# Linear attention on one core: no block and no closing barrier, and the first load in two transfers

## The chip, the cores and the metric

The kernel runs on one core of one Trainium2 chip. The metric is the device time of one execution in microseconds. Each execution also has a *span*, from the first to the last instruction in its trace. The metric is longer than the span; the difference is called "outside the span" below.

## The reference

```python
phi_q = where(q > 0, q + 1, exp(q)) + 1e-6      # q, k, v: 1 x 32 x 2048 x 128, bf16
phi_k = where(k > 0, k + 1, exp(k)) + 1e-6
kv  = einsum("bhsd,bhse->bhde", phi_k, v);  z = phi_k summed over s
out = einsum("bhqd,bhde->bhqe", phi_q, kv) / (einsum("bhqd,bhd->bhq", phi_q, z)[..., None] + 1e-6)
```

## The kernel before

For each of 32 heads, q, k and v come in as one transfer each of 128 rows of 4 KB (512 KB). PE transposes q; ACT takes the exponentials (`eq`, `ek`) and a relu; DVE and POOL do the rest of phi and copy v; PE forms kv and the result; DVE divides; one 512 KB store goes out per head (the last in three parts). Every engine runs a fixed list of operations. SP issues every transfer. These are the parts that the change and the argument touch (`# ...` marks cuts):

```python
WARM = (15, 4, 4)              # warm-up matmuls: w2 and w1 (4 + 4) run before the first transposes
ORDER = {
    "PE": "w2 w1 T0.0 T0.1 w0 kv0.0 kv0.1 ...",
    "SP": "ldq0.0 ldk0.0 ldv0.0 ldk1.0 ldq1.0 ...",
}
# ...
def load(name, dst, src, h, i, t0, t1, last):
    add("SP", f"ld{name}{h}.{i}", lambda e: e.dma_start(dst[:, h % NI, t0:t1], rows(src, h)[:, t0:t1]),
        last, dma=f"{name}{h % NI}.{i}")
# ... the first transposes wait for ldq0 and for the identity that POOL builds
block = es.enter_context(nc.Block())

@block.gpsimd
def _(e):
    pr.emit("POOL", e)

@block.sync
def _(e):
    pr.emit("SP", e)
    for s in range(NO):                       # 12 output buffers; the last store uses o7
        if f"o{s}" in pr.count:
            e.wait_ge(pr.get(f"o{s}"), pr.count[f"o{s}"])
# ... the same for scalar, tensor, vector; the block ends in a drain and a barrier of all engines
```

## Time and profile before

| | before |
|---|---|
| time, median of the first 3 runs | 171.89 us |
| span of the profiled run (its time was 171.16) | 169.3 us |
| last store issued, last landing, end of span | 165.52, 168.53, 169.26 us |

The page begins with the span and the busy time of each engine. PE, DVE and ACT are all above 90%, so no share tells what a change at either end is worth.

```profile
span 169.3 us, 6317 instructions
...
PE 158.8 (94%) x2775; PEld 153.5 (91%) x2775; DVE 153.5 (91%) x267; ACT 153.7 (91%) x133; POOL 85.8 (51%) x71
```

The table of windows gives, for each stretch, its length, the busy time of each engine, the granted clock, the busy share of the DMA engines and what they moved. From 12 us on both ACT and the DMA engines are full; the last two columns of the first rows show how soon the DMA stream gets to speed.

```profile
core 0: us, PE busy (x) PEld busy (x) DVE busy (x) ACT busy (x) POOL busy (x), PEclk, DMA share, GB/s
2.00:3.00 1.00, 1.00 (x4) 0.36 (x3) 0.00 (x0) 0.02 (x1) 0.00 (x0) 1.00 0.92 319
3.00:7.00 4.00, 4.00 (x28) 2.19 (x27) 0.47 (x2) 1.66 (x2) 1.27 (x1) 1.00 1.01 397
7.00:12.00 5.00, 4.86 (x57) 3.43 (x55) 2.88 (x11) 5.00 (x7) 1.79 (x3) 1.00 1.02 415
12.00:150.00 138.00, 136.15 (x2469) 135.42 (x2470) 135.43 (x229) 137.22 (x118) 79.52 (x60) 1.00 1.03 413
```

The timeline of SP's queue at the start (start, duration): each issue keeps the queue for about 0.4 us, and the second load goes out at 1.16. The first packets of q0 move at 1.87.

```profile
0.74 0.37 SPq L324 DMA_DIRECT2D la<-in_q_dram  x1
1.16 0.42 SPq L324 DMA_DIRECT2D la<-in_k_dram  x1
1.63 0.42 SPq L324 DMA_DIRECT2D la<-in_v_dram  x1
```

The timeline at the start, ACT's first activation and POOL's first instruction inside the block (the memset that begins the identity); in brackets, how long the engine had been idle and what ended that. The activation is what the first transposes release.

```profile
0.73 0.20 POOL L300 MEMSET la<- 128x128 bf16 x1 [0.29 <-POOLq L468]
...
5.34 1.02 ACT L372 ACTIVATE la<-la 128x1024 bf16<-128x1024 bf16 x1 [3.32 <-PE la L368]
```

The instructions of SP's closing waits (L442) and of the end of the block (L253): count, duration in ns, first and last start. The last landing is at 168.53; everything that starts after it is what the block's end costs.

```profile
L442 SPq EVENT_SEMAPHORE  x6: 17/28/28, 167.2 to 168.8; - x6
```

```profile
L253 SPq COMPARE_BRANCH  x1: 38/38/38, 168.9 to 168.9; - x1
L253 SPq DRAIN  x1: 7/7/7, 169.0 to 169.0; - x1
L253 SPq EVENT_SEMAPHORE  x1: 17/17/17, 169.2 to 169.2; - x1
L253 ACTq EVENT_SEMAPHORE  x1: 17/17/17, 169.2 to 169.2; - x1
```

### The profile page before, as it was taken

Reading aid. Unit: us, or ns where it says so; the run is one execution under the profiler, and the core shown is the slowest. Engines: PE = TensorE matmul, PEld = TensorE weight load, DVE = VectorE, ACT = ScalarE, POOL = GpSimd, SP = SyncE. Lnnn points to the kernel's source line nnn. Section 1 sums busy time; section 2 is a strip of 40 time slices with the busy share of each in tenths; the row PEclk is TensorE's granted clock in tenths of the full one; section 3 lists DMA queues with packets and bytes.
Section 4 is the critical chain, followed back from the end, with each engine's and each line's share of the span. In section 5 each row is a group of like instructions: output and inputs, shape, how many; then the busy total and the mean of one; then the engine's idle time right before and its main releaser. Section 6 shows DMA issues by size and latency. Waiting matters only on the chain.

```text
span 169.3 us, 6317 instructions
## 1 busy us (share of the span) xinstructions
PE 158.8 (94%) x2775; PEld 153.5 (91%) x2775; DVE 153.5 (91%) x267; ACT 153.7 (91%) x133; POOL 85.8 (51%) x71
## 2 busy tenths in 40 slices
PE   6997999999999999999999999999999999999850
PEld 2576989999999999999999999999999999999740
DVE  0178989999999999999999999999999999999891
ACT  3799989999999999999999999999999999995800
POOL 1446546655665456545566555554565555635000
PEclk9999999999999999999999999999999999999999
DMA  5999999999999999999999999999999999999984
GB/s 204 394 420 415 403 407 410 406 410 410 413 410 410 410 411 407 410 408 419 411 415 417 413 423 411 411 419 408 415 417 414 417 413 419 415 412 420 391 342 175
DMA packets 18748, 67.53 MB, mean 399 GB/s; under 512 B 2080, under 2 KB 2464, under 8 KB 18720
## 3 DMA queue, kind: packets, MB, share of 16 engines
q1 hardware_dynamic: 18720, 67.12, 98.5%
q8 instruction: 22, 0.36, 0.8%
q14 instruction: 6, 0.05, 0.1%
HBM read 50.33 MB, written 16.78 MB: 396 GB/s over the span
## 4 chain that ended last, share of the span: by engine, by line
PE 86%; DVE 6%; ACT 4%; issue 1%; DVEq 0%; POOL 0%; POOLq 0%
PE la L357 33%; PE la L394 19%; PE la L396 17%; PE la L368 15%; DVE la L410 4%; ACT la L336 2%; PE la L315 2%; ACT la L372 1%; PE la L389 1%; DVE la L374 1%; DVE la L403 1%; ACT la L378 1%; DVE la L342 0%; DVEq L253 0%; ACT la L362 0%
## 5 line engine op out<-in xcount | busy, mean ns | idle before, releaser
L410 DVE TENSOR_TENSOR la<-la 128x1536 bf16<-128x1536 f32 (+2 forms) x65 | 77.6, 1195 | 0.3
L396 PE MATMUL la<-la 128*128 128x129 bf16 x512 | 68.1, 220 | 0.0
L394 PE MATMUL la<-la 128*128 128x129 bf16 x512 | 68.1, 219 | 0.0
L372 ACT ACTIVATE la<-la 128x2048 bf16<-128x2048 bf16 (+2 forms) x35 | 60.4, 1731 | 5.0 <-PE la L368 3.3
L357 PE MATMUL la<-la 128*128 128x129 bf16 x1024 | 64.0, 219 | 0.0
L336 ACT ACTIVATE la<-la 128x2048 bf16<-128x2048 bf16 (+1 forms) x33 | 61.3, 1861 | 0.0
L350 POOL COPY la<-la 128x1024 int32<-128x1024 int32 (+1 forms) x33 | 40.3, 1223 | 40.1 <-DVE la L403 30.5
L357 PEld LDWEIGHTS la<-la 128*128 128x128 bf16 x1024 | 60.0, 97 | 0.5 <-POOL la L350 0.5
L346 POOL TENSOR_SCALAR la<-la 128x1024 bf16<-128x1024 bf16 x32 | 44.9, 1403 | 28.2 <-DVE la L410 24.2
L396 PEld LDWEIGHTS la<-la 128*128 128x128 bf16 x512 | 49.5, 97 | 0.0
L394 PEld LDWEIGHTS la<-la 128*128 128x128 bf16 x512 | 47.1, 97 | 0.0
L389 PE MATMUL la<-la 128*128 128x3 bf16 (+1 forms) x192 | 32.3, 168 | 3.4 <-DVE la L410 1.9
L368 PE MATMUL la<-la 128*128 128x128 bf16 x512 | 33.7, 219 | 0.0
L378 ACT ACTIVATE la<-la 128x1024 bf16<-128x1024 bf16 (+1 forms) x32 | 33.5, 1046 | 0.0
L368 PEld LDWEIGHTS la<-la 128*128 128x128 bf16 x512 | 29.2, 97 | 0.9 <-DMA la<-in_q_dram 0.2
L339 DVE TENSOR_SCALAR la<-la 128x2048 bf16<-128x2048 bf16 (+1 forms) x33 | 23.5, 716 | 3.1 <-ACT la L336 3.0
L389 PEld LDWEIGHTS la<-la 128*128 128x128 bf16 x192 | 18.7, 97 | 4.4 <-DVE la L410 2.3
L374 DVE TENSOR_SCALAR la<-la 128x2048 bf16<-128x2048 bf16 (+2 forms) x35 | 21.9, 625 | 0.1
L381 DVE TENSOR_SCALAR la<-la 128x1024 bf16<-128x1024 bf16 x31 | 20.8, 672 | 0.2 <-ACT la L372 0.2
L342 DVE TENSOR_SCALAR la<-la 128x1024 bf16<-128x1024 bf16 x32 | 14.2, 447 | 5.3 <-DMA la<-in_k_dram 5.3
L403 DVE RECIPROCAL la<-la 128x12 f32<-128x12 f32 (+2 forms) x65 | 12.8, 198 | 2.9 <-ACT la L362 1.0
L362 ACT ACTIVATE la<-la 128x129 bf16<-128x129 f32 x32 | 9.0, 282 | 0.8 <-PE la L357 0.8
(14 smaller groups left out, 11.7 us busy)
## 6 DMA issues: line engine op xcount, KB each, us to landing
la<-in_q_dram SPq DMA_DIRECT2D x32, 512.0 KB, 15.4
la<-in_k_dram SPq DMA_DIRECT2D x32, 512.0 KB, 15.3
la<-in_v_dram SPq DMA_DIRECT2D x32, 512.0 KB, 15.4
out_dram<-la SPq DMA_DIRECT2D x31, 512.0 KB, 15.3
out_dram<-la SPq DMA_DIRECT2D x2, 192.0 KB, 2.8
out_dram<-la SPq DMA_DIRECT2D x1, 128.0 KB, 3.0
```

What stands on the lines that cost most here:

```text
L336: add("ACT", f"ek{h}.{i}", lambda e, a=a, b=b: e.activation(em_sb[:, h % NE, a:b], k_sb[:, h % NI, a:b], ACT.Exp), over("ldk", h, ld_parts ...
L346: add("POOL", f"rkp{h}.{i}", lambda e, a=a, b=b: e.tensor_scalar(rk_sb[:, h % NR, a:b], k_sb[:, h % NI, a:b], BIG, 0.0, op0=ALU.min, op1=A ...
L350: add("POOL", f"v1{h}.{i}", lambda e, a=a, b=b: e.tensor_copy(v1_sb[:, h % NV, a:b, 0:D].bitcast(i32), v_sb[:, h % NI, a:b].bitcast(i32)), ...
L357: ins = e.matmul(kv_ps, lhsT=src[:, j], rhs=v1_sb[:, h % NV, j, 0:NC], start=(j + part == 0), stop=(j == NT - 1 and part == 1))
L368: ins = e.transpose(xT[:, j], q_sb[:, h % NI, j], ident[:])
L372: add("ACT", f"eq{h}.{i}", lambda e, a=a, b=b: e.activation(emq_sb[:, h % NQ, a:b], xT[:, a:b], ACT.Exp), over("T", h, t_parts, a, b) + fr ...
L374: add("DVE", f"emq{h}.{i}", lambda e, a=a, b=b: e.tensor_scalar(emq_sb[:, h % NQ, a:b], emq_sb[:, h % NQ, a:b], 1.0, EPS, op0=ALU.min, op1 ...
L378: add("ACT", f"rqa{h}", lambda e: e.activation(rq_sb[:, h % NQ, 0:n], xT[:, 0:n], ACT.Relu), over("T", h, t_parts, 0, n) + freed(NQ, h, (" ...
L389: e.matmul(_ap(o_ps[:, :], o + D, [[NC, m]]), lhsT=ones[:], rhs=epsr[:, 0:m], start=True, stop=False, skip_group_check=True)
L394: e.matmul(to, lhsT=emq_sb[:, h % NQ, t], rhs=kvs_sb[:, h % NK], start=False, stop=False, skip_group_check=True)
L396: ins = e.matmul(to, lhsT=rq_sb[:, h % NQ, t], rhs=kvs_sb[:, h % NK], start=False, stop=True, skip_group_check=True)
L410: return e.tensor_tensor(out=_ap(o_sb[:, :, :, :], first(o_sb[:, h % NO, t0, 0:1]) - first(o_sb[:, :, :, :]), [[m * D, nb], [D, m], [1, D] ...
```

## The change

Its intent: save the branches into and out of the block and the barrier at its end, and let the DMA engines start sooner with a small first transfer (16 of the 128 rows of q0). The waits at the end are put in an order in which the last store's comes last.

```diff
 WARM = (15, 4, 4)
+FIRST = "ldq0.0"
     "SP": """
-        ldq0.0 ldk0.0 ldv0.0 ...
+        first ldq0.0 ldk0.0 ldv0.0 ...
         def load(name, dst, src, h, i, t0, t1, last):
-            add("SP", f"ld{name}{h}.{i}", lambda e: e.dma_start(dst[:, h % NI, t0:t1], rows(src, h)[:, t0:t1]),
+            p0 = 0
+            if f"ld{name}{h}.{i}" == FIRST:
+                p0 = 16
+                add("SP", "first", lambda e: e.dma_start(dst[:p0, h % NI, t0:t1], rows(src, h)[:p0, t0:t1]), dma="first")
+            add("SP", f"ld{name}{h}.{i}", lambda e: e.dma_start(dst[p0:, h % NI, t0:t1], rows(src, h)[p0:, t0:t1]),
                 last, dma=f"{name}{h % NI}.{i}")
 # (the first transposes also wait for "first")
-        block = es.enter_context(nc.Block())
-        @block.gpsimd
-        def _(e):
-            pr.emit("POOL", e)
-        # ... and so on for each engine, with SP's waits for o0 to o11 in that order
+        for e, engine in (("POOL", nc.gpsimd), ("SP", nc.sync), ("ACT", nc.scalar), ("PE", nc.tensor), ("DVE", nc.vector)):
+            pr.emit(e, engine)
+        last = f"o{(NH - 1) % NO}"
+        for name in [f"o{s}" for s in range(NO) if f"o{s}" in pr.count and f"o{s}" != last] + [last]:
+            nc.sync.wait_ge(pr.get(name), pr.count[name])
```

More of the change, by code (lines that the diff above doesn't have):

```diff
@@ L132 @@
     "SP": """
-        ldq0.0 ldk0.0 ldv0.0 ldk1.0 ldq1.0 ldv1.0 ldk2.0 ldk3.0 ldq2.0 ldv2.0 ldq3.0 ldk4.0 ldv3.0 ldv4.0 ldk5.0
+        first ldq0.0 ldk0.0 ldv0.0 ldk1.0 ldq1.0 ldv1.0 ldk2.0 ldk3.0 ldq2.0 ldv2.0 ldq3.0 ldk4.0 ldv3.0 ldv4.0 ldk5.0
         ldq4.0 ldk6.0 ldv5.0 ldq5.0 ldk7.0 ldv6.0 ldv7.0 ldq6.0 ldk8.0 ldq7.0 ldv8.0 ldk9.0 ldq8.0 ldq9.0 ldv9.0
@@ L369, in g @@
                     return ins
-                add("PE", f"T{h}.{i}", g, over("ldq", h, ld_parts, a, b) + ["ident"] + ((every("eq", h - 1, q_parts) + rqs(h - 1)) if h else []))
+                add("PE", f"T{h}.{i}", g, over("ldq", h, ld_parts, a, b) + (["first"] if h == 0 else []) + ["ident"] + ((every("eq", h - 1, q_parts) + rqs(h - 1)) if h else []))
             for i, (a, b) in enumerate(q_parts(h)):
@@ L430, in bass_standalone__linear_attn_elu__prompt_kernel @@
             pr.get(name)
-        block = es.enter_context(nc.Block())
-        @block.gpsimd
-        def _(e):
-            pr.emit("POOL", e)
-        @block.sync
-        def _(e):
-            pr.emit("SP", e)
-            for s in range(NO):
-                if f"o{s}" in pr.count:
-                    e.wait_ge(pr.get(f"o{s}"), pr.count[f"o{s}"])
-        @block.scalar
-        def _(e):
-            pr.emit("ACT", e)
-        @block.tensor
-        def _(e):
-            pr.emit("PE", e)
-        @block.vector
-        def _(e):
-            pr.emit("DVE", e)
+        for e, engine in (("POOL", nc.gpsimd), ("SP", nc.sync), ("ACT", nc.scalar), ("PE", nc.tensor), ("DVE", nc.vector)):
[3 more added lines that the diff above has]
+            nc.sync.wait_ge(pr.get(name), pr.count[name])
 _INS = ['q', 'k', 'v']
```

## The prediction

> **What bounds the kernel now.** Time 171.89 us; profiled span 169.3. In the table of windows, from 12 to 150 us, ACT is busy 137.2 of 138 us, PE 136.2, and the DMA engines move 413 GB/s without a pause. At the start the chain of waits is: POOL builds the identity (0.73 to 1.47), eight warm-up matmuls (3.33 us), the first transposes at 4.7, ACT's first activation at 5.34; ACT then hardly stops until 160.2. The first load (q0) is issued at 0.74, its first packets move at 1.87, its last landing is at 4.08: 0.1 to 0.2 us before the warm-up lets the transposes start. At the end DVE stops at 165.5; the last store, issued at 165.52, lands at 168.53. The last stores land every 1.25 us, the slowest DMA engine never idle, so DMA sets the end as much as DVE.
>
> **What the change removes, adds and moves.**
>
> 1. End. SP sees the last landing at 168.55. Then come four waits already satisfied (0.06 each), a compare-and-branch at 168.87, a drain at 169.04 and a five-engine barrier to 169.26: 0.71 us, all on the critical path. The change puts the last store's wait last and has no branch, drain or barrier, so the span should end within 0.05 us of the last landing. Gain 0.7 us. The runtime's own wait for all engines ("Runtime: NRT & Kernel Launch", the preamble/postamble breakdown, about 1.5 us) stays, outside the span; this trace does not show it. The metric is some 2 us longer than the span, so I assume that it counts the program's end and passes the 0.7 us on.
>
> 2. Start, branches. Between the opening barrier's release (SP 0.67, POOL 0.63) and the first issue (0.74) or memset (0.73) stands one branch. Without it I expect 0.03 to 0.08 us earlier on both; POOL's is on the path through the warm-up to ACT.
>
> 3. Start, the split. The first issue took 0.37 us; packets started 1.13 us after it began. Estimate: 16 rows still cost 0.2 to 0.35 us of issue, since stores of 1, 1.5 and 4 KB rows all take 0.33. The first packets come perhaps 0.1 to 0.2 us earlier, for 64 KB (0.16 us at 410 GB/s), but the 112 rows and all later loads are issued 0.2 to 0.35 us later, their packets at about 2.1. "DMA: Bandwidth & Descriptors" (section on the semaphore increment of 16, how many engines) gives the largest common divisor up to 16, so both parts use all 16 engines. The stream's opening packets are slow (205 to 411 ns against 159); the small transfer may absorb that. Net on the DMA stream: -0.2 to +0.15 us. One more wait for the first transposes, free unless q0 lands after 4.2.
>
> Nothing else changes order. On the critical path lie 0.7 us at the end and about 0.1 at the start.
>
> **Prediction: 171.0 us, 8 in 10 between 170.5 and 171.6.** Faster by over 2%: 0.01; within 2%: 0.98; slower: 0.01.
>
> **What would show it.** Span about 168.5; no drain or barrier after the last landing; POOL's memset and SP's issue 0.03 to 0.08 us earlier; first packets at 1.6 to 1.8; q0 landed at 3.9 to 4.2; first activation at 5.25 to 5.3; last landing 168.2 to 168.6.
>
> **What would make it wrong.** The time may exclude the closing barrier, leaving 0.1 us. The second issue may delay the bulk and so q0 past the warm-up. The instruction-fetch packets (22 of 16 KB, about 1.05 us each) may fall on other DMA engines and move the last landing by up to 1 us either way.

## More of the kernel before

The waits of ACT from 100 to 165 us (total, times, longest): one, and it is for PE. No activation waits for a load.

```profile
ACT la L372 <- PE la L396: 1.7, 1, 1.7
```

## The result

| | before | after |
|---|---|---|
| time, median of 6 runs each | 171.84 us | 171.25 us |
| time, mean of the same runs | 171.71 us | 171.21 us |
| span, mean (after: the same 6 runs; before: 11 runs, whose mean time is 171.68) | 169.83 us | 169.88 us |
| outside the span (mean time less mean span of the same runs) | 1.85 us | 1.33 us |

The ratio is 0.9971, with a 95% interval of 0.9947 to 0.9995: a small gain, within 2%. The interval only just excludes 1. A ratio here is the mean time of one kernel's runs over that of the other's of the same rounds, so it is not quite the ratio of the medians.

The time falls, by 0.5 to 0.6 us where the prediction had 0.9 (171.89 to 171.0), but the span does not fall at all. It was to be 168.5 us. And the part outside the span, which the prediction held constant, fell by 0.52 us. The profiled runs are not a pair: before's is one of its fastest (171.16), after's one of its slower (171.51), so their spans differ by 0.9 us while the means are equal.

```profile
span 170.2 us, 6307 instructions
...
PE 159.8 (94%) x2775; PEld 153.9 (90%) x2775; DVE 154.6 (91%) x267; ACT 153.9 (90%) x133; POOL 85.0 (50%) x71
```

The windows of after: from 2 to 3 us the DMA engines move 135 GB/s instead of 319, from 3 to 7 us 342 instead of 397, from 7 to 12 us 399 instead of 415. Only then are the streams alike.

```profile
core 0: us, PE busy (x) PEld busy (x) DVE busy (x) ACT busy (x) POOL busy (x), PEclk, DMA share, GB/s
2.00:3.00 1.00, 1.00 (x4) 0.35 (x3) 0.00 (x0) 0.01 (x1) 0.00 (x0) 1.00 0.64 135
3.00:7.00 4.00, 4.00 (x25) 2.32 (x24) 0.47 (x2) 1.10 (x2) 0.91 (x1) 1.00 1.01 342
7.00:12.00 5.00, 4.89 (x55) 3.40 (x54) 2.76 (x9) 5.00 (x5) 1.73 (x3) 1.00 1.01 399
12.00:150.00 138.00, 135.60 (x2453) 134.37 (x2451) 135.05 (x228) 136.62 (x116) 77.85 (x60) 1.00 1.03 413
```

SP's queue after: the 16 rows take as long to issue as 128 did, and k0 goes out at 1.64 instead of 1.16.

```profile
0.74 0.39 SPq L328 DMA_DIRECT2D la<-in_q_dram  x1
1.18 0.42 SPq L329 DMA_DIRECT2D la<-in_q_dram  x1
1.64 0.42 SPq L329 DMA_DIRECT2D la<-in_k_dram  x1
```

The timeline at the start: POOL's memset has not moved, nor has SP's first issue, so the branches into the block cost nothing that a trace shows. ACT's first activation is 0.56 us later in this pair of profiles. Only 0.13 us of it is the later q0 (the transposes begin at 4.83 instead of 4.70); the rest is PE's pace, as will be seen.

```profile
0.73 0.20 POOL L301 MEMSET la<- 128x128 bf16 x1 [0.29 <-POOLq L454]
...
5.90 1.02 ACT L377 ACTIVATE la<-la 128x1024 bf16<-128x1024 bf16 x1 [3.89 <-PE la L373]
```

The closing waits: the last of them ends the span, 0.04 us after the last landing (170.16), and nothing of the block's end is left. (The count is x6 in both; an instruction can wait for two semaphores.)

```profile
L440 SPq EVENT_SEMAPHORE  x6: 28/28/28, 168.8 to 170.2; - x6
```

ACT's waits from 100 to 165 us: there is a new one, for a load of k (at 146 us).

```profile
ACT la L377 <- PE la L401: 1.9, 1, 1.9
ACT la L341 <- DMA la<-in_k_dram: 0.7, 1, 0.7
```

So a first accounting: the end gained more than was predicted, and something at the start gave part of it back. The landings of some transfers, first and last of the 16 DMA engines, from the trace (us), show how long the loss lasts:

| transfer | before: first, last engine | after: first, last engine |
|---|---|---|
| q0 (after: the 112 rows) | 3.67, 4.08 | 4.37, 4.78 |
| k0 | 4.97, 5.32 | 5.62, 6.02 |
| the tenth load after q0 | 16.53, 18.56 | 17.46, 19.25 |
| store of head 22 | 152.30, 157.21 | 153.12, 158.85 |

The engine that is first is 0.7 to 1.0 us later in after from 8 us on to the stores near the end: the DMA engines show no idle share in between (1.01 to 1.03), and what the stream loses in the first microseconds it does not make up in this pair. How far the last engine trails varies more from profile to profile.

### The profile page after: what moved, and what is told of

It is laid out like the page before. It is cut to its first block, busy times and chain, and to the rows that moved or that the text cites. A ratio compares the mean times of both kernels' runs of the same rounds, so it can differ in the third digit from the quotient of the medians. Undisturbed runs are those within 1.5% of the kernel's fastest.

```text
span 170.2 us, 6307 instructions
## 1 busy us (share of the span) xinstructions
PE 159.8 (94%) x2775; PEld 153.9 (90%) x2775; DVE 154.6 (91%) x267; ACT 153.9 (90%) x133; POOL 85.0 (50%) x71
## 4 chain that ended last, share of the span: by engine, by line
ACT 64%; PE 16%; DMA 10%; DVE 7%; POOL 1%; issue 1%; SPq 0%; POOLq 0%; DVEq 0%
ACT la L341 24%; ACT la L377 24%; ACT la L383 12%; DMA la<-in_k_dram 10%; DVE la L415 4%; PE la L362 4%; ACT la L367 3%; PE la L399 3%; PE la L401 3%; PE la L373 3%; PE la L316 2%; DVE la L408 1%; POOL la L355 1%; DVE la L347 1%; PE la L394 1%
## 5 line engine op out<-in xcount | busy, mean ns | idle before, releaser
L355 POOL COPY la<-la 128x1024 int32<-128x1024 int32 (+1 forms) x33 | 39.6, 1200 | 42.4 <-DVE la L408 27.9
L373 PE MATMUL la<-la 128*128 128x128 bf16 x512 | 34.4, 221 | 0.1
L344 DVE TENSOR_SCALAR la<-la 128x2048 bf16<-128x2048 bf16 (+1 forms) x33 | 25.2, 766 | 2.7 <-ACT la L341 2.6
L347 DVE TENSOR_SCALAR la<-la 128x1024 bf16<-128x1024 bf16 x32 | 15.1, 474 | 6.9 <-DMA la<-in_k_dram 6.9
L379 DVE TENSOR_SCALAR la<-la 128x2048 bf16<-128x2048 bf16 (+2 forms) x35 | 21.1, 602 | 0.1
L386 DVE TENSOR_SCALAR la<-la 128x1024 bf16<-128x1024 bf16 x31 | 20.8, 671 | 0.1
```

The source lines that it names most:

```text
L344: add("DVE", f"em{h}.{i}", lambda e, a=a, b=b: e.tensor_scalar(em_sb[:, h % NE, a:b], em_sb[:, h % NE, a:b], 1.0, EPS, op0=ALU.min, op1=AL ...
L355: add("POOL", f"v1{h}.{i}", lambda e, a=a, b=b: e.tensor_copy(v1_sb[:, h % NV, a:b, 0:D].bitcast(i32), v_sb[:, h % NI, a:b].bitcast(i32)), ...
L373: ins = e.transpose(xT[:, j], q_sb[:, h % NI, j], ident[:])
```

## The experiments

**Theory A.** The split costs time, because a 16-row issue holds SP's queue as long as a full one and every later load goes out 0.45 us later; the end gains more than 0.7 us, because part of the gain lies outside the span. **Rival B** (the prediction): the split is neutral and the end gains only what the result shows. Twelve runs of eleven kernels were made, each with before beside it. All outputs are right. In the table, "us to before" is the mean of the kernel's 6 executions less the mean of before's 11 (a plus or minus in the text is an estimate, two standard errors from these executions); "outside" is time less span; "after landing" is from the last landing to the end of the span, in the profiled run.

| kernel | median us | ratio (95% interval) | us to before | outside | after landing |
|---|---|---|---|---|---|
| before (three calls) | 171.69, 171.68, 171.72 | 1 | 0 | 1.85, 1.85, 1.87 | 0.73 |
| the change | 171.25 | 0.9971 (0.9947 to 0.9995) | -0.50 | 1.33 | 0.04 |
| no_split | 170.87 | 0.9942 (0.9915 to 0.9969) | -0.96 | 1.33 | 0.04 |
| no_split_again | 170.28 | 0.9933 (0.9909 to 0.9957) | -1.32 | 1.31 | 0.04 |
| split_only | 172.49 | 1.0038 (1.0014 to 1.0062) | +0.76 | 1.89 | 0.73 |
| waits_only | 171.33 | 0.9983 (0.9959 to 1.0008) | -0.26 | 1.90 | 0.47 |
| barrier_back | 171.30 | 0.9982 (0.9962 to 1.0002) | -0.28 | 1.83 | 0.30 |
| all_wait | 171.09 | 0.9971 (0.9951 to 0.9991) | -0.49 | 1.90 | 0.08 |
| two_queues | 170.88 | 0.9954 (0.9937 to 0.9970) | -0.79 | 1.37 | 0.04 |
| tiny_first | 170.94 | 0.9959 (0.9940 to 0.9979) | -0.69 | 1.30 | 0.04 |
| warm_more | 171.16 | 0.9969 (0.9953 to 0.9985) | -0.53 | 1.30 | 0.04 |
| col_split | 171.05 | 0.9957 (0.9934 to 0.9981) | -0.78 | 1.30 | 0.04 |
| half_rows | 171.29 | 0.9986 (0.9961 to 1.0012) | -0.28 | 1.33 | 0.04 |
| warm_less | 170.86 | 0.9946 (0.9925 to 0.9966) | -0.98 | 1.30 | 0.04 |

### no_split: the change without its split

```diff
-        first ldq0.0 ldk0.0 ldv0.0 ...
+        ldq0.0 ldk0.0 ldv0.0 ...
-FIRST = "ldq0.0"
+FIRST = None
 (and the first transposes no longer wait for "first")
```

> The change without its split: no block, no barrier, last store waited for last, the first load whole. Theory A (the split costs, the end gains more than its 0.7 us): first packets at 1.87 us, q0 landed at about 4.1, first activation at 5.34 as before; span about 168.6 (0.7 below before); time 1.1 to 1.4 us below before, that is about 170.6, since the part of the time outside the span also shrank (1.9 us before, 1.3 after). Rival B (the split is neutral, as I predicted, and the end gains only 0.6 in all): time within 0.2 us of the changed kernel, 0.6 below before, ratio about 0.9965.

Measured: 0.96 us below before (expected 1.1 to 1.4), and 1.32 in the repeat; q0 landed at 4.15. The part outside the span is 1.33, as in the change. This run alone does not exclude rival B: its ratio of 0.9965 lies inside the interval (0.9915 to 0.9969). The repeat (0.9909 to 0.9957) excludes it, and so does split_only. The first activation was at 5.80, not 5.34, though q0 was there: see "What moved the first activation" below.

### split_only: before with the split alone

```diff
-        ldq0.0 ldk0.0 ldv0.0 ...
+        first ldq0.0 ldk0.0 ldv0.0 ...
 (and the load and the transposes' wait as in the change; block and closing barrier stay)
```

> The kernel before with the split of the first load alone; block and closing barrier stay. Theory A: the stream of loads starts one issue (0.44 us) later and opens slowly; q0 lands at about 4.8, first activation at about 5.9, last landing 0.5 to 0.8 us later than in the run of before, time 0.5 to 0.8 us above before (about 172.5). Rival B: q0 still lands at 4.1 to 4.3, time within 0.15 us of before.

Measured: 0.76 us above before, the interval clear of 1; q0 landed at 4.99, the first activation was at 6.10, the last landing at 170.19. This is the split's cost by itself, and rival B falls. It agrees with the other pair: no_split is 1.14 below before (mean of the two), the change 0.50, so the split costs 0.64 there (plus or minus 0.5). The stream opens slowly here too (windows), and activations wait for k as in after (ACT's waits, 100 to 165 us):

```profile
2.00:3.00 1.00, 1.00 (x4) 0.34 (x3) 0.00 (x0) 0.01 (x1) 0.00 (x0) 1.00 0.68 193
3.00:7.00 4.00, 3.87 (x24) 2.21 (x23) 0.47 (x2) 0.90 (x1) 0.44 (x1) 1.00 0.94 312
```

```profile
ACT la L341 <- DMA la<-in_k_dram: 0.8, 2, 0.5
```

### waits_only: before with the closing waits reordered

```diff
-            for s in range(NO):
-                if f"o{s}" in pr.count:
-                    e.wait_ge(pr.get(f"o{s}"), pr.count[f"o{s}"])
+            last = f"o{(NH - 1) % NO}"
+            for name in [f"o{s}" for s in range(NO) if f"o{s}" in pr.count and f"o{s}" != last] + [last]:
+                e.wait_ge(pr.get(name), pr.count[name])
```

> The kernel before with only the order of the closing waits changed (the last store's last). The four satisfied waits of 0.06 us each move ahead of the last landing: gain 0.2 to 0.3 us in the span after the last landing (0.73 before, about 0.45 here), time 0.2 to 0.3 below before under both theories; if the gain lay in the order of waits alone, 0.6 or more.

Measured: 0.26 below before, and 0.47 instead of 0.73 after the last landing: the four satisfied waits are worth 0.26 us, as expected. The interval reaches 1.0008, so the time alone would not prove it; the trace does.

### barrier_back: no_split with a barrier at the end

```diff
             nc.sync.wait_ge(pr.get(name), pr.count[name])
+        nc.all_engine_barrier()
```

> no_split with an explicit barrier of all engines put back after the last wait (still no block, so no branches). Theory A: from the last landing to the end of the span about 0.4 us, the part of the time outside the span back to about 1.9 us, so the time 0.9 to 1.1 us above no_split, close to waits_only. If the branches and not the barrier were what cost, the time would stay within 0.2 us of no_split.

Measured: 0.69 above no_split (0.86 above both its runs together, plus or minus 0.43), less than the 0.9 to 1.1 expected. I had put the barrier at 0.4 us and it ends the span 0.30 us after the last landing, which is 0.1 of the gap; the part outside the span is back at 1.83, not 1.9; the rest is within the noise. The time equals that of waits_only, which has block and branches as well. In the traces the block's end takes 0.17 us more than the bare barrier (0.47 against 0.30: the compare-and-branch and the drain), which the times do not resolve. So before's 0.73 us after the last landing are 0.26 of waits, 0.17 of branch and drain, 0.26 of barrier and 0.04 that stay.

### all_wait: no barrier, but every engine waits for the last store

```diff
             nc.sync.wait_ge(pr.get(name), pr.count[name])
+        for engine in (nc.gpsimd, nc.scalar, nc.tensor, nc.vector):
+            engine.wait_ge(pr.get(last), pr.count[last])
```

> no_split with all five engines waiting for the last store's landing, and no barrier. Theory A (the part of the time outside the span is the engines' closing work, which four engines get done early when they need not wait for the last store): span as in no_split, within 0.1 us of the last landing, but the part outside the span rises from 1.33 to about 1.85, time 0.5 above no_split. Rival (the barrier itself costs that part): it stays at 1.33, time as no_split.

Measured: no barrier, and the span ends 0.08 us after the last landing, but the part outside the span is 1.90 again, and the time is 0.47 us above no_split's first run (0.83 above its second; the runs are from different calls). So the 0.5 us outside the span is not the barrier's own cost: it depends on when the other four engines reach the end of their programs. "Runtime: NRT & Kernel Launch" in the Trainium skill, in its preamble/postamble breakdown, lists for after the kernel a wait for all engines and a reset of 51 semaphores per engine. That each engine does a share of its own as soon as its program ends would fit the numbers, though the page lists the wait before the reset; no trace here shows what runs outside the span, and only the dependence is shown.

### two_queues: the 16 rows from ACT's queue

```diff
-                add("SP", "first", lambda e: ...
+                add("ACT", "first", lambda e: ...      # first in ACT's order, no longer in SP's
```

> The changed kernel with the 16-row transfer issued from ACT's queue at the same time as SP issues the 112 rows. Theory A1 (the split costs because the 16-row issue takes 0.39 us of SP's queue, as long as a full one, and pushes every other load back by 0.44): the cost goes; SP's next load (k0) is issued at 1.17 again, q0 lands at 4.0 to 4.3 instead of 4.8 to 5.0, k0 at 5.3; time like no_split, about 0.5 to 0.6 below split_only less the end's gain, ratio to before about 0.994. Theory A2 (the small transfer's packets and the second semaphore cost): the loads still land 0.5 or more late, ratio about 0.997.

Measured: SP issues k0 at 1.18 as A1 asked, but q0's parts landed at 3.86 and 4.66 and k0 at 5.84, late, and activations still waited for k late in the run (0.7 us in all). The ratio, 0.9954, lies between the two forecasts, and its interval overlaps those of the change and of no_split, so the time decides nothing. The landings do: with SP's queue free the loads are late all the same, so A1 alone is not enough. SP's queue, and the window from 3 to 7 us, in which this kernel moves what the changed one does:

```profile
0.74 0.39 SPq L329 DMA_DIRECT2D la<-in_q_dram  x1
1.18 0.42 SPq L329 DMA_DIRECT2D la<-in_k_dram  x1
```

```profile
3.00:7.00 4.00, 4.00 (x28) 2.12 (x27) 0.47 (x2) 1.56 (x2) 1.08 (x1) 1.00 1.02 342
```

### tiny_first: the issue without the cut

```diff
-        ldq0.0 ldk0.0 ldv0.0 ...
+        tiny ldq0.0 ldk0.0 ldv0.0 ...
+        scratch = sb([16, 256])
+        add("SP", "tiny", lambda e: e.dma_start(scratch[:], rows(qf, 1)[:16, 0:2].rearrange("p j d -> p (j d)")), dma="tiny")
```

> no_split with a transfer of 16 rows of 512 B (8 KB, to a scratch tile nobody reads) issued ahead of the whole first load: the issue without the bytes of the split. A1: its issue takes 0.35 to 0.4 us, q0 is issued at 1.17, q0 lands 0.4 to 0.7 later than in no_split (4.6 to 4.8), time 0.4 to 0.7 above no_split. A2: q0 lands as in no_split, same time.

Measured: 8 KB take 0.39 us to issue, the whole q0 goes out at 1.18 and lands at 4.54, 0.39 later than in no_split. So one more issue ahead of the stream delays it by itself, as A1 says. That it costs time is not shown: the mean is 0.27 above no_split's first run and 0.63 above its second (0.45 plus or minus 0.45 together), and the last landing of its profile, 169.46, is that of no_split's first, 169.48. The stream then runs at full speed, unlike in the kernels that cut q0 (SP's queue, then the window):

```profile
0.74 0.39 SPq L428 DMA_DIRECT2D la<-in_q_dram  x1
1.18 0.41 SPq L329 DMA_DIRECT2D la<-in_q_dram  x1
```

```profile
3.00:7.00 4.00, 4.00 (x23) 2.56 (x22) 0.47 (x2) 1.21 (x2) 1.09 (x1) 1.00 1.02 401
```

### warm_more and warm_less: the other path through the start

```diff
-WARM = (15, 4, 4)
+WARM = (15, 4, 6)      # warm_more;  (15, 4, 3) in warm_less; both on top of no_split
```

> no_split with 10 instead of 8 warm-up matmuls ahead of the first transposes; the loads are untouched. If the end is set by when PE lets ACT start, the first activation moves from 5.34 to 5.8 to 5.9 to 6.3 and the time rises by 0.3 to 0.8 us over no_split. If the end is set by the DMA stream (the slowest of its engines is never idle), the time stays within 0.2 us of no_split and the last landing with it, and the cost of the split is that of the loads, not of the later first transposes.

Measured: the first activation at 6.26 (0.46 later), the time 0.43 us above no_split's first run and 0.79 above its second (0.61 plus or minus 0.38 together). The loads were untouched, so the compute chain from the first transposes on sets the time as well. The forecast for a pure DMA bound (within 0.2) fails over both runs together; the first alone would not settle it.

> no_split with 7 instead of 8 warm-up matmuls before the first transposes, which may then start at 4.3 instead of 4.7, about when q0 has landed (4.1). If the start of the compute chain still governs (two more matmuls cost 0.46 us), the first activation comes at 5.4 instead of 5.8 and the time falls 0.2 to 0.4 us below no_split, to about 170.5; if the DMA stream holds the end, it stays within 0.15 us.

Measured: the first activation came at 5.40, but the time was not below no_split: 0.34 above it on the same chip, intervals overlapping (0.9925 to 0.9966, 0.9909 to 0.9957). So a later start of compute costs, and no gain from an earlier one is seen. The second half is weak: the transposes began at 4.30 instead of 4.70, but at PE's slow pace (16 in 1.91 us, see below), so that compute started hardly earlier than in the faster profile of no_split (5.32). That start of compute and DMA stream are close to balanced is a reading that fits, not one that is shown.

### col_split and half_rows: other cuts of q0

> The changed kernel with the same 64 KB first, but cut across the rows' length: 128 rows of 512 B, then 128 rows of 3584 B[...]. Theory M (two queues and tiny first showed that the issue slot is only part of the cost; the rest is that 112 rows give each engine 7 rows, other ones than the 8 of a whole load, and the engines get in each other's way: 0.32 to 0.35 MB per us from 3 to 7 us against 0.40): here 0.38 to 0.41 MB per us from 3 to 7 us, 3.7 to 3.9 MB moved by 12 us (3.50 in the changed kernel), no packets of 1.4 us and over; time 0.1 to 0.3 us above no_split, ratio to before 0.994 to 0.996. Rival I (two transfers cost the same however they are cut): 3.5 MB by 12 us, ratio 0.997.

```diff
-                p0 = 16
-                add(... dst[:p0, h % NI, t0:t1], rows(src, h)[:p0, t0:t1] ...)     # then rows p0 to 127
+                c0 = 2
+                add(... dst[:, h % NI, t0:c0], rows(src, h)[:, t0:c0] ...)         # then columns c0 to t1
```

Measured: theory M fails. With 128 rows in both parts, as in a whole load (no trace shows which rows an engine serves), from 3 to 7 us the stream still moves 344 GB/s, there are two packets of 1.4 us at 5.06, and 3.51 MB are moved by 12 us, as rival I said (3.95 in before). (Such long packets are no mark of the cut: warm_more and warm_less, with q0 whole, have one of 1.4 us each before 5 us.) The time, 0.78 below before, is better than the changed kernel's, but the intervals overlap.

> The changed kernel with the first load cut at row 64 instead of row 16: 64 and 64 rows, 4 per engine. Theory M: the rows of an engine again differ from those of a whole load, so a slow stretch as in the changed kernel: 0.30 to 0.37 MB per us from 3 to 7 us, 3.4 to 3.7 MB by 12 us, ratio to before 0.996 to 0.998. Rival I': only the issue slot costs, and 256 KB first hide it (0.64 us of moving against 0.44 us of issue): 3.9 MB by 12 us, ratio 0.994.

```diff
-                p0 = 16
+                p0 = 64
```

Measured: 326 GB/s from 3 to 7 us, 3.51 MB by 12 us, and a ratio of 0.9986, the worst of the cuts with the change's end. In its profile the first three issues took 0.57 us each instead of 0.4 (SP's queue below, then the window; the reason is open), so it does not tell theory M from rival I; only "256 KB first hide the issue" is refuted.

```profile
0.73 0.57 SPq L328 DMA_DIRECT2D la<-in_q_dram  x1
1.36 0.57 SPq L329 DMA_DIRECT2D la<-in_q_dram  x1
```

```profile
3.00:7.00 4.00, 3.60 (x25) 1.76 (x24) 0.14 (x1) 1.03 (x2) 0.08 (x1) 1.00 1.00 326
```

Over all profiles, from 3 to 7 us: the eight of kernels that load q0 whole and first show 353 to 397 GB/s (mean 376), the five of kernels that cut it 312 to 344 (mean 333), the one with a tiny transfer ahead 401. An estimate from the means: 43 GB/s less over 4 us is 0.17 MB, at 413 GB/s some 0.4 us. Why a cut load disturbs the stream is open: SP's queue alone does not explain it (two_queues), nor does the number of rows in a part (col_split).

### no_split_again

> no_split once more, on the chip of the three others, for the ratios: 0.9942 to before the first time; I expect 0.993 to 0.996, part outside the span 1.3 us, 3.8 to 3.95 MB moved by 12 us.

Measured: 0.9933, 1.31 outside the span, 3.82 MB by 12 us. This is the fastest kernel in both of its calls, 0.9942 and 0.9933 of before against 0.9971 for the change. It was run at another time. The second interval (0.9909 to 0.9957) and the change's (0.9947 to 0.9995) overlap by 0.001.

### What moved the first activation

In nine of the profiles the first transposes start at 4.67 to 4.71, at the end of the eight warm-up matmuls, and yet the first activation comes anywhere from 5.32 to 5.80. The difference is the pace of PE, in the timelines of before and of barrier_back:

```profile
4.70 1.06 PE L368 MATMUL la<-la 128*128 128x128 bf16 x16
```

```profile
4.70 1.91 PE L373 MATMUL la<-la 128*128 128x128 bf16 x16
```

The same 16 transposes take 1.06 us in one profile and 1.91 in the other. In the traces the spacing of PE's matmuls halves (transposes from 107 to 56 ns) within 0.2 us of the moment at which the clock record kept with each trace turns to full: 4.68 us in before, 6.12 in after, 6.02 in no_split, 4.64 in its repeat, 7.32 in barrier_back. "TensorE: Matmul & The Clock Gate" in the Trainium skill, part 1, says that PE starts at half clock and goes to the full one after a free-running window of about 3.4 us, so that the moment varies from run to run. The traces agree that it varies (here the full clock came 3.1 to 5.8 us after the warm-up's start at 1.53); two profiles of one kernel, no_split, differ, so it is luck and not the change, and it moves the compute chain of single runs by about half a microsecond. The granted clock in the table of windows reads 1.00 in all of them and shows nothing of this. It is a good reason not to subtract one profile from another.

How such a lag reaches the end can be followed along ACT. In twelve of the fourteen profiles the last store is issued 7.2 us after ACT's last activation (7.35 and 7.40 in the others). Against its repeat, no_split's ACT is 0.48 us late from the first activation, and 1.48 late from 23 us on, after a longer wait for PE and none for a load; it stays so to the end (last landing 169.48 against 168.53). The changed kernel is 0.49 us behind the same repeat at 22 us, 0.82 from 29 us and 1.58 after its wait for k at 146. The lines are of no_split, of its repeat, and of after:

```profile
23.30 0.28 ACT L367 ACTIVATE la<-la 128x129 bf16<-128x129 f32 x1 [1.54 <-PE la L362]
```

```profile
21.82 0.28 ACT L367 ACTIVATE la<-la 128x129 bf16<-128x129 f32 x1 [0.50 <-PE la L362]
```

```profile
146.44 1.91 ACT L341 ACTIVATE la<-la 128x2048 bf16<-128x2048 bf16 x1 [0.65 <-DMA la<-in_k_dram]
```

The twelve executions of no_split fall into two groups, six at 169.87 to 170.30 us and six at 170.83 to 171.22, and its two profiles are one of each; the six of the change lie at 170.77 to 171.60. So the split may cost mainly the chance of the faster group. That is a reading of few executions, and why the wait at 23 us is long in seven of the nine profiles that load q0 whole was not traced.

## Why the prediction was right, and which of its steps were not

The time is inside the range (171.25; predicted 171.0, 170.5 to 171.6). Of its terms, two were wrong by more than half a microsecond each, and they offset each other. That the sum came out close is luck, not understanding: the mechanism at the end was right, the one at the start was not.

| step, as the prediction put it | predicted us | measured us |
|---|---|---|
| 1. end, after the last landing ("Gain 0.7 us") | -0.7 | -0.69 (0.73 to 0.04): 0.26 order of the waits, 0.17 branch and drain, 0.26 barrier |
| 1. "The metric is some 2 us longer than the span, so I assume that it counts the program's end and passes the 0.7 us on" | 0 outside the span | -0.52 (1.85 to 1.33) |
| 2. branches: "0.03 to 0.08 us earlier on both" | -0.03 to -0.08 | 0.00 (SP 0.738 to 0.737, POOL 0.733 to 0.731) |
| 3. split: "Net on the DMA stream: -0.2 to +0.15 us" | about 0 | +0.76 (split_only), +0.64 (the change against no_split) |
| sum | about -0.8 | about -0.5; measured -0.50 |

- **The end** was right in the span, and the metric did pass the 0.7 us on; what failed is the assumption that nothing else changes there. Without a common end the other four engines finish early, worth another 0.5 us (all_wait takes it away again without any barrier). The end alone is then worth 1.21 us, and no_split measures 1.14.
- **The branches**: I took the gap of 0.07 us between the opening barrier and the first issue for a branch. The gap is as long without one.
- **The split** is the step that failed. I saw that a 16-row issue could cost 0.2 to 0.35 us; it cost 0.39, which is as much as a full one. The prediction then let an earlier start of the stream and "the small transfer may absorb that" pay for it. The first packets came at 1.76, but those of whole loads come at 1.73 to 1.87 in the other profiles, so nothing was gained there, and the stream did worse from 2 to 12 us, for two reasons: the issue slot (in tiny_first it alone makes q0 land 0.39 us later) and a slow stretch in every kernel that cuts q0. And "One more wait for the first transposes, free unless q0 lands after 4.2" set the limit too early: with q0 at 4.54 the transposes still began at 4.70 (tiny_first), with 4.66 at 4.71 (two_queues), and with the changed kernel's 4.78 at 4.83, so that wait cost 0.13 us. How much of the 0.7 us reaches the end by late compute and how much by late loads is not settled over the means; late compute alone was shown to cost (warm_more), late loads alone were not (tiny_first), though in the changed kernel's profile the wait for k makes up 0.76 of ACT's lag.
- "DMA: Bandwidth & Descriptors" in the Trainium skill (how many engines) was used for both parts running on all 16 DMA engines. The traces agree: 16 landings for each part.
- "Span about 168.5" and "last landing 168.2 to 168.6" failed with step 3: the mean span was 169.88, the last landing of the profiled run 170.16. Whether the instruction fetches moved single landings was not tested.

## What to carry to other kernels

Don't end all engines together: a barrier at the end cost its own 0.26 us here (a wait that every engine shares, 0.04), and either cost another 0.5 us outside the span; let one engine wait for the last store, and wait for that store last. A transfer's issue cost the same 0.4 us for 16 rows as for 128, so a small transfer ahead of a saturated stream delayed the stream, and here the stream did not catch up. When a change has two parts, run each alone: here the sum hid a gain of 1.2 us and a loss of 0.7.

## What the Trainium skill lacked or had wrong

- "Runtime: NRT & Kernel Launch" (preamble/postamble breakdown) gives the closing stages as fixed costs. That some of it seems to leave the critical path when engines end early is missing: 1.30 to 1.37 us outside the span where only SP waits, 1.83 to 1.90 where all engines do.
- "DMA: Bandwidth & Descriptors" gives no time for the issue of a transfer by its size on this chip. Here, with no backlog: 0.39 us for 16 rows of 512 B, 0.39 for 16 rows of 4 KB, 0.37 for 128 rows of 4 KB (and, unexplained, 0.57 for 64 rows in the one profile of half_rows). Nor has any page a number for the slow stretch after a first load cut in two (312 to 344 GB/s from 3 to 7 us, against 353 to 397).
- "Perfetto Trace Analysis" (DMA Instruction, HWDGE) says that the generator of descriptors is locked for exclusive use while an issue's descriptors are made. In two_queues ACT's issue (0.73 to 1.15 us) and SP's (0.74 to 1.13) ran at the same time and took 0.42 and 0.39 us, about as long as an issue alone. No serialization is to be seen; a lock held for a small part of the 0.4 us would not show.
- "TensorE: Matmul & The Clock Gate" (part 1) puts the change of clock at around 4 us into sustained activity, within 500 ns from run to run. Warm-up began at 1.53 us here, and the clock record turned to full between 4.64 and 7.33 us over the profiles: 3.1 to 5.8 us in.
